# Weight conversion moved to two batches' tiles, an order edge on VectorE, and 18 identity products on TensorE

## The chip, the cores and the metric

One core of one Trainium2 chip runs the kernel. The metric is the time of the whole program on the device in microseconds. A profile is one further execution with the hardware profiler on.

## The reference, cut to what matters

```
a = softmax(phi) over the 32 slots            # (4, 8, 576, 32)
k_m, v_m = a^T k, a^T v                       # per head: 32 x 64
attn = softmax(q k_m^T / 8) v_m               # (4, 8, 576, 64)
x  = attn as 2304 tokens x 512
y1 = relu(x @ w_in)^2 @ w_out                 # first MLP,  512 -> 2048 -> 512
h  = y1 @ w_in2
out = (h * tanh(softplus(h))) @ w_out2        # second MLP, 512 -> 2048 -> 512
```

q, k, v and phi are float32; the four weight matrices arrive as 64-bit floats.

## The kernel before, in words

**Weights.** Class `Conv` turns a weight matrix into float32 in 16 units of 128 x 512 ("i1" is the first MLP's input matrix, "o1" its output matrix, "i2" and "o2" those of the second MLP). A unit takes: one load of 512 KB of raw words (L167, issued by SyncE, three buffers), a Prelu on ScalarE (L192) that scales the high word, a shift on VectorE (L214), a shift-or on VectorE (L221); for all but i1 also the split into a rounded high part on ScalarE (L187, type fp32r) and the low part on VectorE (L229). One `tick` starts a unit, does the bit operations of the unit started a tick earlier and the split of the one before that. Units of o1 stay in SBUF. Units of i2 and o2 are written from a staging tile (pool Y, tag `i1`, four buffers) to DRAM (L231) and read back later by `load_w2` (L713). The four buffers of tag `i1` are also those of the weight pages of the first input matrix: its halves `win` and the weight pages `win1r` that `load_page` (L592) reads back from DRAM.

**First MLP with attention.** `attn_unit` computes the softmax of 288 tokens of one batch ("half") and leaves it as high part `ah` (ScalarE, L375) and low part `al` (VectorE, L376). `w_part` (L386 to L393) multiplies v_m into two 128-column blocks of w_in, which gives `wp`, also as high and low part. `a_tile` then does, for each of a range of 16 blocks `fc`: six products `h` (L471 to L473) of 288 columns, Relu and Square on ScalarE (L479, L480), the split `g` into two parts (L484 or L486 on ScalarE or, for batch 3, VectorE; L487 on VectorE), and three blocks later (LAG) twelve products into four accumulators `a` (L433 to L435). `evac_y1` stores y1 to DRAM.

Batches 0 and 1 share their weights: twelve `a_tile` calls (blocks 0 to 3, 4 to 9, 10 to 15, each for both batches and both halves). They are called the first, second and third group below. Then come batch 2, halves 0 and 1, and batch 3, halves 0 and 1, with all 16 blocks each. Beside these products run the attention of later halves and the memory of later batches (`kv_unit`), a step per block. The converter `c1` (i1 and o1) runs in the first two groups; `c2` (first all of i2, then all of o2) in the third group and in batch 2, with a start in two of three ticks. In batch 3 nothing is converted; i2 is read back from DRAM in its first half, o2 in its second.

**Second MLP.** 2304 tokens in five tiles of 512 or 384, 16 blocks each: twelve products `hb` (L780 to L782), the activation on three engines, twelve or nine products `b` (L755 to L757).

**Order of the work.** A planner orders each engine's instructions by a simulated time line, so program order is not the order on the engine. `behind(marks, key)` adds an edge: the instructions in its block stand behind the marked one on the same engine. `c1.after` places the converter's VectorE work behind `marks[b, half]`; `kv_soft` of batch 2 (the maximum of phi, L260) stands behind `marks[1, 1]`. With `paced`, a Prelu stands behind the last Relu. All loads and stores are issued by SyncE, in one queue in its order. Each engine runs its own queue in order.

Of the kernel before, what the change touches and what calls it, by code (L numbers as in the profile page):

```python
# [8 lines left out]
F32 = mybir.dt.float32  # L9
F32R = mybir.dt.float32r  # L10
# [7 lines left out]
B, H, S, D, M = 4, 8, 576, 64, 32  # L18
DM, FF = 512, 2048
P = 128  # L20
# [4 lines left out]
NF = FF // P  # L25
# [4 lines left out]
LAG = 3  # L30
# [5 lines left out]
def body(tc, q, kvm, kvt, phi, w_in1, w_out1, w_in2, w_out2, out):  # L36
    nc = tc.nc
# [94 lines left out]
    wt = {}  # L132

    w1 = dram.tile([NPG, P, 4, 256], F32, name="w_i1")
    w2 = {key: dram.tile([NF, P, 2, 512], F32, name=f"w_{key}") for key in ("i2", "o2")}

# [11 lines left out]
    class Conv:  # L150
# [20 lines left out]
        def tick(self, start=True, between=None):  # L171


            ends = [x for x in self.flight if x[2] == 2]
            bits = [x for x in self.flight if x[2] == 1]
            for x in ends:
                key, u = x[0], x[1]
                if key[1] == "2":
                    x[4] = Y.tile([P, 2, 512], F32R, tag="i1", name=f"st_{key}_{u}", bufs=4)
                    x[4] = [x[4][:, 0], x[4][:, 1], x[4]]  # L180
                else:
                    if (key, u // 2) not in wt:
                        wt[key, u // 2] = tuple(
                            wo.tile([P, 2, DM], F32R, tag=f"wo{part}{u // 2}", name=f"{key}{part}{u // 2}")
                            for part in "hl")
                    x[4] = [w[:, u % 2, :] for w in wt[key, u // 2]]
                nc.scalar.copy(x[4][0], x[3])  # L187
            if start and self.started < min(self.loaded, self.limit) and self.ready(*self.order[self.started]):
                key, u = self.order[self.started]
                high = self.raw[key, u][:, :, 1].bitcast(F32)  # L190
                with behind(marks, "step" if self.paced else None):
                    nc.scalar.activation(high, high, AF.Prelu, scale=2.0 ** -112, alpha=-2.0 ** 32)  # L192
                self.started += 1
                self.flight.append([key, u, 0, None, None])
            with behind(marks, self.after):
                self.fields(bits, ends, between)
            for x in self.flight:
                x[2] += 1
            for x in list(self.flight):
                if x[2] == 3 or (x[2] == 2 and x[0] == "i1"):  # L200
                    self.done.add((x[0], x[1]))
                    self.flight.remove(x)

        def fields(self, bits, ends, between):
            for x in bits:
                key, u, c = x[0], x[1], x[1] % 2
                if key == "i1":
                    if c == 0:
                        wt[key, u // 2] = Y.tile(
                            [P, 4, 256], F32, tag="i1", name=f"win1_{u // 2}", bufs=4)  # L210
                    x[3] = wt[key, u // 2][:, :, c * P:(c + 1) * P]
                else:
                    x[3] = X.tile([P, 512], F32, tag="ct", name=f"ct_{key}_{u}", bufs=2)
                nc.vector.tensor_scalar(  # L214
                    out=x[3].bitcast(I32), in0=self.word(x, 0), scalar1=29, scalar2=None,
                    op0=ALU.logical_shift_right)
            if between is not None:
                between()
            for x in bits:
                d = x[3].bitcast(I32)  # L220
                nc.vector.scalar_tensor_tensor(  # L221
                    out=d, in0=self.word(x, 1), scalar=3, in1=d,
                    op0=ALU.logical_shift_left, op1=ALU.bitwise_or)
                if x[0] == "i1" and x[1] % 2:
                    nc.sync.dma_start(w1[x[1] // 2], wt["i1", x[1] // 2])
                self.raw.pop((x[0], x[1]))
                self.load()
            for x in ends:
                nc.vector.tensor_sub(x[4][1], x[3], x[4][0].bitcast(F32))  # L229
                if x[0][1] == "2":  # L230
                    nc.sync.dma_start(w2[x[0]][x[1]], x[4][2].bitcast(F32))  # L231

        def word(self, x, i):
            t = self.raw[x[0], x[1]][:, :, i]
# [8 lines left out]
    def bank(tag, name):  # L243
        return psum.tile([P, 512], F32, tag=tag, name=name)
# [10 lines left out]
    def kv_soft(b, p):  # L255

        ph = phi_t[p][:, at[p]:at[p] + S]
        mx = Y.tile([P, 1], F32, tag="mx", name=f"mx{b}{p}", bufs=2)
        with behind(marks, (1, 1) if b == 2 else None):
            nc.vector.tensor_reduce(out=mx, in_=ph, op=ALU.max, axis=AX.X, negate=True)  # L260
        rc = Y.tile([P, 1], F32, tag="rc", name=f"rc{b}{p}", bufs=2)
        nc.scalar.activation(ph, ph, AF.Exp, bias=mx, accum_out=rc)
        rc_t[p] = rc
# [75 lines left out]
    def attn_unit(b, half, nxt=None):  # L339
# [13 lines left out]
        for p in range(2):  # L353
# [11 lines left out]
        nc.vector.tensor_mul(xv, xv, sm.unsqueeze(2).to_broadcast([P, 2 * TB, NB]))  # L365
        yield
        a = Y.tile([P, 2, T], F32, tag="at", name=f"at{n}", bufs=1)
        marks[b, half] = nc.vector.transpose(
            a.rearrange("p a t -> p (a t)"), x.rearrange("p a t -> p (a t)"))
        pool = Y if b in (1, 2) else X  # L370
        a_t[b, half] = tuple(
            pool.tile([P, 2, T], F32R, tag=f"a{part}", name=f"a{part}{b}{half}", bufs=2)
            for part in "hl")
        hi, lo = a_t[b, half]
        nc.scalar.copy(hi, a)  # L375
        nc.vector.tensor_sub(lo, a, hi.bitcast(F32))  # L376
        yield

    wp = {}
# [1 line left out]
    def w_part(b, j, lo, hi):  # L381

        ps = banks2(f"pw{b}{j}{lo}")[:, :, :hi - lo]
        for g in range(4):
            for p in range(2):
                nc.tensor.matmul(  # L386
                    ps[M * g:M * g + M, p], vT[b][D * p:D * p + D, M * g:M * g + M],
                    wt["i1", j][D * p:D * p + D, g, lo:hi], start=True, stop=True)
        if (b, j) not in wp:
            wp[b, j] = page([P, 2, 2, 256], F32R, f"wp{b}{j}")  # L390
        t = wp[b, j]
        nc.scalar.copy(t[:, 0, :, lo:hi], ps)
        nc.vector.tensor_sub(t[:, 1, :, lo:hi], ps, t[:, 0, :, lo:hi].bitcast(F32))  # L393
# [45 lines left out]
    def evac_y1(b, half, first, last):  # L439
# [15 lines left out]
                nc.sync.dma_start(y1[:, dm - 1:dm + 1, c0:c0 + T], y1s[slot, dm // 2])  # L455
        return f

    def a_tile(b, half, f0, f1, tick, mid, post, banks=("mm",)):

        acc = [psum.tile([P, 512], F32, tag=f"acc{d}", name=f"a{b}{half}{f0}{d}") for d in range(4)]  # L460
# [2 lines left out]
        for fc in range(f0, f1):  # L463
# [4 lines left out]
            key = ahead.get((b, half, fc))  # L468
            for hg in range(2):
                with behind(done_pe, key if hg == 0 else None):  # L470
                    nc.tensor.matmul(ph, w[:, 0, hg, fs], hi[:, hg], start=(hg == 0), stop=False)  # L471
                nc.tensor.matmul(ph, w[:, 0, hg, fs], lo[:, hg], start=False, stop=False)  # L472
                nc.tensor.matmul(ph, w[:, 1, hg, fs], hi[:, hg], start=False, stop=(hg == 1))  # L473
            tick(fc)
            flush()
# [41 lines left out]
    for _ in range(N_WARM):  # L517
        nc.tensor.matmul(warm[:, :P], ident, ident, start=True, stop=True)

    kv_soft(0, 0)  # L520
    kv_soft(0, 1)
    kv_turn(0, 0, ("acc0", "acc1"))
# [10 lines left out]
    kv_mem(0, 1, (1,), "acc0")  # L533
    c1.tick()
    kv_heads(0, (1,), "acc1")
    next(at00)
    w_part(0, 0, 0, P)
    next(at00)
    c1.tick()
    c1.after = (0, 0)  # L540
# [29 lines left out]
    def attn_later(b, half):  # L570
        def nxt():
# [11 lines left out]

    subs = [(f0, f1, b, half) for f0, f1 in zip(bounds, bounds[1:])
            for b in range(2) for half in range(2)]
    c2 = Conv([("i2", u) for u in range(NF)] + [("o2", u) for u in range(NF)],
              lambda i: (Y, "raw", 3))

    def load_page(j):

# [4 lines left out]
    for i, (f0, f1, b, half) in enumerate(subs):  # L595
# [26 lines left out]
        def tick(fc):  # L622
            if len(c1.done) < 2 * NF:
                c1.tick()
            elif f0 == bounds[-2]:
                if not c2.loaded:
                    c2.load(3)
                c2.tick(start=fc % 3 != 2)

        def mid(fc):  # L630
            run_step(lanes, n_steps)
# [29 lines left out]


    def tick2(fc):
        c2.tick(start=fc % 3 != 2)

    b, nb = 2, 3
    lanes = [attn_later(b, 1), [[iter(range(2)), 2]] + kv_later(nb)]
# [25 lines left out]
    drain(*lanes)  # L693


    while len(c2.done) < 2 * NF:
        c2.tick()
    close(cm_psum2)
    cm_psum2 = tc.tile_pool(name="psum3", bufs=1, space=PSUM)
# [5 lines left out]
        tiles.append((c, n))  # L705
        c += n

    def load_w2(key, u):
        if key == "i2":
            t = Y2.tile([P, 2, 512], F32R, name=f"i2_{u}")  # L710
        else:
            t = wo.tile([P, 2, 512], F32R, tag=f"wo{'hl'[u % 2]}{u // 2}", name=f"o2_{u}")
        nc.sync.dma_start(t.bitcast(F32), w2[key][u])  # L713
        wt[key, u] = t

    y_raw, y_t = {}, {}

# [12 lines left out]
        nc.scalar.copy(hi, t)  # L730
        (nc.gpsimd if i else nc.vector).tensor_sub(lo, t, hi.bitcast(F32))  # L731

    def post0(fc):
        load_w2("i2", fc)

    def post1(fc):
        if fc >= 8 and fc % 2 == 0:
            load_y(0, fc // 2 - 4)
        elif fc >= 8:
            split_y(0, fc // 2 - 4)  # L740
        if fc >= LAG + 1 and fc % 2 == 0:
            load_w2("o2", fc - LAG - 1)
            load_w2("o2", fc - LAG)

    nothing = lambda fc: None
    acc_tags = ["mm", "b0", "bg1", "bg2"]
    a_tile(B - 1, 0, 0, NF, nothing, nothing, post0, acc_tags)
    a_tile(B - 1, 1, 0, NF, nothing, nothing, post1, acc_tags)


    def mm4_step(acc, fc, gh, gl, n, done):
# [18 lines left out]
    for i, (c0, n) in enumerate(tiles):  # L770
        acc = [psum.tile([P, 512], F32, tag=f"acc{d}", name=f"b{i}{d}") for d in range(n // P)]
        done = store_out(c0)
        for fc in range(NF):
# [9 lines left out]
            if step == 1:  # L783
                flush()
                run_pend(0)
                for c in range(NF):
                    if ("o2", c) not in wt:
                        load_w2("o2", c)
            u = X.tile([P, 512], F32, tag="ah", name=f"u{m}", bufs=2)[:, :n]
            nn = X.tile([P, 512], F32, tag="al", name=f"n{m}", bufs=2)[:, :n]  # L790
            nh = X.tile([P, 512], F32, tag="ys0", name=f"nh{m}", bufs=2)[:, :n]
# [80 lines left out]
```

## Time and profile before

| | |
|---|---|
| three runs | median 811.53 us, from 810.93 to 815.98 |
| profiled execution | 809.73 us, its span 807.9 us |
| mean granted TensorE clock | 0.983 |
| busy share: TensorE, weight load, VectorE, ScalarE, GpSimd | 96%, 84%, 72%, 56%, 15% |

The span in 40 slices of about 20 us; digits are tenths:

```profile
PE   5797999999988999999999999999999999999997
DVE  4988646785677883334588887888878887777774
PEclk7698999999999999999999999999999999999999
DMA  9991435699789977506630002000110001001001
```

PE is TensorE, DVE VectorE, ACT ScalarE, POOL GpSimd, SP SyncE. PEclk is the granted clock: whole at 2.4 GHz, half at 1.2 GHz. TensorE is below nine tenths in the first two slices, in the fourth, in slices twelve and thirteen, and in the last. The two MLPs meet at about 397 us.

### The profile page before, as it was taken

Reading aid. Unit: us, or ns where it says so; the run is one execution under the profiler, and the core shown is the slowest. Engines: PE = TensorE matmul, PEld = TensorE weight load, DVE = VectorE, ACT = ScalarE, POOL = GpSimd, SP = SyncE. Lnnn points to the kernel's source line nnn. Section 1 sums busy time; section 2 is a strip of 40 time slices with the busy share of each in tenths; the row PEclk is TensorE's granted clock in tenths of the full one; section 3 lists DMA queues with packets and bytes.
Section 4 is the critical chain, followed back from the end, with each engine's and each line's share of the span. In section 5 each row is a group of like instructions: output and inputs, shape, how many; then the busy total and the mean of one; then the engine's idle time right before and its main releaser. Section 6 shows DMA issues by size and latency. Waiting matters only on the chain.

```text
span 807.9 us, 13777 instructions
## 1 busy us (share of the span) xinstructions
PE 776.5 (96%) x5288; PEld 676.5 (84%) x5288; DVE 577.8 (72%) x1022; ACT 452.3 (56%) x916; POOL 119.4 (15%) x104
## 2 busy tenths in 40 slices
PE   5797999999988999999999999999999999999997
PEld 4586898999777988999988888888888889999896
DVE  4988646785677883334588887888878887777774
ACT  3767766785657775334445445444564446555453
POOL 0000000000000000000223243222522242222222
PEclk7698999999999999999999999999999999999999
DMA  9991435699789977506630002000110001001001
GB/s 337 406 391 73 164 100 162 235 329 362 251 312 345 389 253 281 211 1 228 248 105 1 0 27 73 0 1 1 39 53 1 0 20 54 1 1 39 1 2 39
DMA packets 38705, 111.77 MB, mean 138 GB/s; under 512 B 3952, under 2 KB 10096, under 8 KB 38640
## 3 DMA queue, kind: packets, MB, share of 16 engines
q1 hardware_dynamic: 38640, 110.90, 37.8%
q8 instruction: 41, 0.67, 0.3%
q14 instruction: 24, 0.20, 0.1%
HBM read 80.48 MB, written 30.41 MB: 137 GB/s over the span
## 4 chain that ended last, share of the span: by engine, by line
PE 80%; DMA 8%; DVE 7%; ACT 3%; issue 1%; SPq 0%; ACTq 0%; DVEq 0%
PE hb L781 8%; PE hb L780 8%; PE hb L782 8%; PE b L756 8%; PE b L755 8%; PE b L757 8%; PE a L433 6%; PE a L435 6%; PE a L434 6%; DMA raw_i<-in_moe_w_in_dram 3%; PE h L471 3%; PE h L472 3%; PE h L473 3%; DMA w_i<-st_i 2%; PE pw L386 1%
## 5 line engine op out<-in xcount | busy, mean ns | idle before, releaser
L433 PE MATMUL a<-g,o1h 128*128 128x288 f32 x512 | 150.3, 301 | 3.0 <-ACT g L484 1.5
L434 PE MATMUL a<-g,o1l 128*128 128x288 f32 x512 | 149.2, 297 | 0.0
L808 POOL TENSOR_TENSOR gl<-nh,gh 128x512 fp32r<-128x512 f32 (+1 forms) x80 | 97.4, 1219 | 285.5 <-PE b L757 177.0
L435 PE MATMUL a<-g,o1h 128*128 128x288 f32 x512 | 134.8, 295 | 0.7 <-DVE g L487 0.7
L781 PE MATMUL hb<-yl,i 128*128 128x512 f32 (+1 forms) x320 | 118.9, 372 | 0.0
L780 PE MATMUL hb<-yh,i 128*128 128x512 f32 (+1 forms) x320 | 118.9, 372 | 0.0
L782 PE MATMUL hb<-yh,i 128*128 128x512 f32 (+1 forms) x320 | 118.8, 371 | 0.0
L804 DVE SCALAR_TENSOR_TENSOR n<-n,u 128x512 f32<-128x512 f32 (+1 forms) x80 | 79.5, 994 | 52.5 <-ACT u L800 52.5
L756 PE MATMUL b<-o,gh 128*128 128x512 f32 x288 | 113.6, 395 | 0.0
L755 PE MATMUL b<-o,gh 128*128 128x512 f32 x288 | 113.5, 394 | 0.0
L757 PE MATMUL b<-o,gl 128*128 128x512 f32 x288 | 112.4, 395 | 0.0
L433 PEld LDWEIGHTS a<-g,o1h 128*128 128x128 f32 x512 | 96.5, 189 | 11.1 <-ACT g L484 4.0
L794 ACT ACTIVATE u<-hb 128x512 f32<-128x512 f32 (+1 forms) x80 | 44.4, 555 | 107.5 <-PE hb L782 107.5
L434 PEld LDWEIGHTS a<-g,o1l 128*128 128x128 f32 x512 | 96.8, 189 | 1.3 <-issue 1.2
L479 ACT ACTIVATE s<-h 128x288 f32<-128x288 f32 x128 | 52.0, 410 | 79.9 <-PE h L473 78.4
L435 PEld LDWEIGHTS a<-g,o1h 128*128 128x128 f32 x512 | 90.7, 188 | 3.0 <-DVE g L487 1.6
L471 PE MATMUL h<-ah,wp 128*128 128x288 f32 x256 | 79.9, 313 | 5.3 <-ACT s L479 2.6
L472 PE MATMUL h<-al,wp 128*128 128x288 f32 x256 | 77.8, 304 | 5.3 <-DVE al L376 5.3
L487 DVE TENSOR_TENSOR g<-s,g 128x288 fp32r<-128x288 f32 x128 | 59.9, 469 | 32.2 <-ACT g L484 30.3
L731 POOL TENSOR_TENSOR yl<-yr,yh 128x512 fp32r<-128x512 f32 (+1 forms) x16 | 21.3, 1345 | 396.2 <-PE h L473 391.4
L807 ACT CAST gh<-nh 128x512 fp32r<-128x512 f32 (+1 forms) x80 | 46.3, 579 | 57.4 <-DVE nh L806 54.3
L473 PE MATMUL h<-ah,wp 128*128 128x288 f32 x256 | 77.1, 301 | 0.0
(98 smaller groups left out, 1393.4 us busy)
## 6 DMA issues: line engine op xcount, KB each, us to landing
raw_i<-in_moe_w_in_dram SPq DMA_DIRECT2D x32, 512.0 KB, 5.2
raw_o<-in_moe_w_out_dram SPq DMA_DIRECT2D x32, 512.0 KB, 7.7
win1r<-w_i SPq DMA_DIRECT2D x17, 512.0 KB, 5.8
w_i<-st_i SPq DMA_DIRECT2D x16, 512.0 KB, 4.5
w_o<-st_o SPq DMA_DIRECT2D x16, 512.0 KB, 6.8
i<-w_i SPq DMA_DIRECT2D x16, 512.0 KB, 7.7
o<-w_o SPq DMA_DIRECT2D x16, 512.0 KB, 4.1
kv<-in_kvm_dram SPq DMA_DIRECT2D x5, 1024.0 KB, 8.8
```

Source lines behind the costliest of these rows:

```text
L433: nc.tensor.matmul(o, wh[:, c, cs], sh, start=first, stop=False)
L434: nc.tensor.matmul(o, wl[:, c, cs], sh, start=False, stop=False)
L435: nc.tensor.matmul(o, wh[:, c, cs], sl, start=False, stop=last)
L471: nc.tensor.matmul(ph, w[:, 0, hg, fs], hi[:, hg], start=(hg == 0), stop=False)
L472: nc.tensor.matmul(ph, w[:, 0, hg, fs], lo[:, hg], start=False, stop=False)
L473: nc.tensor.matmul(ph, w[:, 1, hg, fs], hi[:, hg], start=False, stop=(hg == 1))
L755: nc.tensor.matmul(acc[t], gh[:, cs], wh, start=(fc == 0), stop=False)
L756: nc.tensor.matmul(acc[t], gh[:, cs], wl, start=False, stop=False)
L757: nc.tensor.matmul(acc[t], gl[:, cs], wh, start=False, stop=(fc == NF - 1))
L780: nc.tensor.matmul(h, wh[:, d * P:d * P + P], yh, start=(d == 0), stop=False)
L781: nc.tensor.matmul(h, wh[:, d * P:d * P + P], yl, start=False, stop=False)
L782: nc.tensor.matmul(h, wl[:, d * P:d * P + P], yh, start=False, stop=(d == 3))
```

## The change

i2 and o2 are no longer converted by one converter. `c2` converts o2 alone, in the tiles of batch 2, a start every second block; its first three loads are issued in the last `a_tile` of the third group. Its staging tiles are two tiles of 128 x 512 (one for each part) under the tags `ys2` and `ys3` of pool Y, two buffers each, and each part is stored by a DMA of its own. A new converter `c3` converts i2 in the tiles of batch 3, straight into the SBUF tiles that the second MLP reads; the DRAM copy of i2, its stores and its read-back are gone. Both are paced. `marks[b, half]` is now the low part `al` (L376) and no longer the transpose before it (L368). `keep_warm` issues products of the identity with itself behind a given TensorE instruction: four behind a transpose of `kv_heads`, five behind the first `w_part`, five and four behind the first two products of the first `a_tile`.

```
-    w2 = {key: dram.tile([NF, P, 2, 512], F32, name=f"w_{key}") for key in ("i2", "o2")}
+    w2 = dram.tile([NF, P, 2, 512], F32, name="w_o2")
...
-                if key[1] == "2":
-                    x[4] = Y.tile([P, 2, 512], F32R, tag="i1", name=f"st_{key}_{u}", bufs=4)
-                    x[4] = [x[4][:, 0], x[4][:, 1], x[4]]
+                if key == "i2":
+                    t = wt[key, u] = Y2.tile([P, 2, 512], F32R, name=f"i2_{u}")
+                    x[4] = [t[:, 0], t[:, 1]]
+                elif key == "o2":
+                    x[4] = [Y.tile([P, 512], F32R, tag=f"ys{i}", name=f"st{i}_{u}", bufs=2) for i in (2, 3)]
...
-                if x[0][1] == "2":
-                    nc.sync.dma_start(w2[x[0]][x[1]], x[4][2].bitcast(F32))
+                if x[0] == "o2":
+                    for i in range(2):
+                        nc.sync.dma_start(w2[x[1], :, i], x[4][i].bitcast(F32))
...
-        marks[b, half] = nc.vector.transpose(
-            a.rearrange("p a t -> p (a t)"), x.rearrange("p a t -> p (a t)"))
+        nc.vector.transpose(a.rearrange("p a t -> p (a t)"), x.rearrange("p a t -> p (a t)"))
...
-        nc.vector.tensor_sub(lo, a, hi.bitcast(F32))
+        marks[b, half] = nc.vector.tensor_sub(lo, a, hi.bitcast(F32))
...
+    def keep_warm(ins, n):
+        with tc.issue_after(ins.ins):
+            for _ in range(n):
+                nc.tensor.matmul(warm2[:, :P], ident, ident, start=True, stop=True)
...
+                if n == "00_0" and hg == 0:
+                    keep_warm(one, 5)
...
+                if n == "00_0" and hg == 0:
+                    keep_warm(one, 4)
...
+    keep_warm(done_pe["pkt", 0], 4)
     next(at00)
     w_part(0, 0, 0, P)
+    keep_warm(done_pe["pw"], 5)
...
-    c2 = Conv([("i2", u) for u in range(NF)] + [("o2", u) for u in range(NF)],
-              lambda i: (Y, "raw", 3))
+    c2 = Conv([("o2", u) for u in range(NF)], lambda i: (Y, "raw", 3))
+    c3 = Conv([("i2", u) for u in range(NF)], lambda i: (Y2, "raw", 3))
+    c2.paced = c3.paced = True
...
-            elif f0 == bounds[-2]:
-                if not c2.loaded:
-                    c2.load(3)
-                c2.tick(start=fc % 3 != 2)
+            elif final and not c2.loaded:
+                c2.load(3)
...
     def tick2(fc):
-        c2.tick(start=fc % 3 != 2)
+        c2.tick(start=fc % 2 == 0)
...
+    c3.load(3)
+
+    def tick3(fc):
+        c3.tick(start=fc % 2 == 0)
...
-    def post0(fc):
-        load_w2("i2", fc)
...
-    a_tile(B - 1, 0, 0, NF, nothing, nothing, post0, acc_tags)
-    a_tile(B - 1, 1, 0, NF, nothing, nothing, post1, acc_tags)
+    a_tile(B - 1, 0, 0, NF, tick3, nothing, nothing, acc_tags)
+    a_tile(B - 1, 1, 0, NF, tick3, nothing, post1, acc_tags)
+    while len(c3.done) < NF:
+        c3.tick()
```

## Rows read from the trace of the kernel before

**Rows 1.** Windows by stage: stretch, its length, busy us (instructions) by engine, clock, DMA, GB/s

```profile
...
70.96:83.16 12.20, 7.97 (x52) 7.16 (x53) 11.03 (x26) 8.63 (x22) 0.00 (x0) 0.72 0.16 51
...
150.44:221.53 71.09, 68.84 (x635) 63.02 (x633) 46.80 (x101) 48.42 (x114) 0.00 (x0) 1.00 0.86 305
221.53:277.46 55.93, 50.02 (x513) 44.02 (x513) 45.04 (x92) 38.10 (x85) 0.00 (x0) 1.00 0.93 341
277.46:320.31 42.85, 42.85 (x407) 38.20 (x406) 25.27 (x49) 29.96 (x70) 0.00 (x0) 1.00 0.77 287
...
358.58:396.77 38.19, 38.19 (x291) 38.19 (x289) 16.79 (x38) 18.30 (x42) 3.90 (x4) 1.00 0.58 206
396.77:807.90 411.13, 406.64 (x1862) 342.75 (x1860) 324.86 (x484) 204.41 (x352) 114.61 (x93) 1.00 0.08 27
```

**Rows 2.** Chain of waits, 220 to 262 us: start, us, what

```profile
...
225.07 7.06 DMA w_i<-st_i
...
247.67 9.32 DMA w_o<-st_o
257.07 0.62 ACT st_o L187
...
258.54 0.40 PE h L471
...
```

**Rows 3.** Waits of ScalarE, 150.4 to 277.5 us: who for whom, us, times, longest

```profile
ACT raw_o L192 <- DMA raw_o<-in_moe_w_out_dram: 8.3, 4, 2.8
ACT raw_i L192 <- DMA raw_i<-in_moe_w_in_dram: 7.1, 8, 1.6
...
ACT st_o L187 <- DMA w_o<-st_o: 4.5, 2, 3.8
...
```

**Rows 4.** Time line of TensorE, 70 to 81 us: start, us, instruction, idle before it

```profile
70.96 0.53 PE L471 MATMUL h<-ah,wp 128*128 128x288 f32 x2 [0.37 <-ACT ah L375]
75.72 0.61 PE L472 MATMUL h<-al,wp 128*128 128x288 f32 x1 [4.23 <-DVE al L376]
...
80.87 0.66 PE L386 MATMUL pw<-win,vT 64*32 64x256 f32 x16
```

**Rows 5.** Time line of VectorE, 69 to 79 us

```profile
69.43 0.78 DVE L368 STREAM_TRANSPOSE at<-x 128x576 f32<-128x576 f32 x1
...
72.04 1.41 DVE L260 TENSOR_REDUCE mx<-phi 128x1 f32<-128x576 f32 x2
...
74.92 0.75 DVE L376 TENSOR_TENSOR al<-at,ah 128x576 fp32r<-128x576 f32 x1
...
78.33 0.69 DVE L221 SCALAR_TENSOR_TENSOR win<-raw_i,win 128x512 int32<-128x512 int32 x1 [0.50 <-ACT raw_i L192]
```

**Rows 6.** Windows of the two stretches at half clock

```profile
12.00:32.48 20.48, 12.17 (x164) 7.99 (x165) 17.54 (x37) 11.61 (x24) 0.00 (x0) 0.50 1.04 403
...
73.44:80.27 6.83, 4.55 (x19) 4.55 (x20) 6.14 (x17) 4.56 (x13) 0.00 (x0) 0.50 0.07 27
```

**Rows 7.** Time line of TensorE at the start

```profile
1.52 3.78 PE L518 MATMUL warm<-ident 128*128 128x128 f32 x16 [1.52 <-POOL ident masks.py:199]
...
22.42 0.61 PE L471 MATMUL h<-ah,wp 128*128 128x288 f32 x1 [1.14 <-ACT wp L392]
...
24.13 0.61 PE L472 MATMUL h<-al,wp 128*128 128x288 f32 x1 [1.10 <-DVE al L376]
```

**Rows 8.** A conversion unit's instructions: durations in ns, least/median/most

```profile
L192 ACT ACTIVATE raw_i<-raw_i x32: 651/676/705, 12.6 to 190.4; 128x512 f32<-128x512 f32 x32
...
L187 ACT CAST st_i<-ct_i x16: 604/622/637, 143.5 to 228.6; 128x512 fp32r<-128x512 f32 x16
...
L214 DVE TENSOR_SCALAR ct_i<-raw_i x16: 417/422/429, 140.8 to 222.2; 128x512 int32<-128x512 int32 x16
L221 DVE SCALAR_TENSOR_TENSOR ct_i<-raw_i,ct_i x16: 682/686/695, 141.8 to 222.9; 128x512 int32<-128x512 int32 x16
L229 DVE TENSOR_TENSOR st_i<-ct_i,st_i x16: 681/688/694, 145.2 to 229.6; 128x512 fp32r<-128x512 f32 x16
```

More of the change, by code (lines that the diff above doesn't have):

```diff
@@ L385, in w_part @@
             for p in range(2):
-                nc.tensor.matmul(
+                done_pe["pw"] = nc.tensor.matmul(
                     ps[M * g:M * g + M, p], vT[b][D * p:D * p + D, M * g:M * g + M],
@@ L470, in a_tile @@
                 with behind(done_pe, key if hg == 0 else None):
-                    nc.tensor.matmul(ph, w[:, 0, hg, fs], hi[:, hg], start=(hg == 0), stop=False)
-                nc.tensor.matmul(ph, w[:, 0, hg, fs], lo[:, hg], start=False, stop=False)
+                    one = nc.tensor.matmul(ph, w[:, 0, hg, fs], hi[:, hg], start=(hg == 0), stop=False)
+                if n == "00_0" and hg == 0:
+                    keep_warm(one, 5)
+                one = nc.tensor.matmul(ph, w[:, 0, hg, fs], lo[:, hg], start=False, stop=False)
+                if n == "00_0" and hg == 0:
+                    keep_warm(one, 4)
                 nc.tensor.matmul(ph, w[:, 1, hg, fs], hi[:, hg], start=False, stop=(hg == 1))
@@ L518, in body @@
         nc.tensor.matmul(warm[:, :P], ident, ident, start=True, stop=True)
+    warm2 = bank("b0", "warm2")
     kv_soft(0, 0)
@@ L693, in body @@
     drain(*lanes)
-    while len(c2.done) < 2 * NF:
+    while len(c2.done) < NF:
         c2.tick()
@@ L706, in body, with load_w2 @@
         c += n
[L708 to L714, printed above, removed]
+    def load_w2(u):
+        t = wo.tile([P, 2, 512], F32R, tag=f"wo{'hl'[u % 2]}{u // 2}", name=f"o2_{u}")
+        nc.sync.dma_start(t.bitcast(F32), w2[u])
+        wt["o2", u] = t
+    c3.load(3)
+    def tick3(fc):
+        c3.tick(start=fc % 2 == 0)
     y_raw, y_t = {}, {}
@@ L741, in post1 @@
         if fc >= LAG + 1 and fc % 2 == 0:
-            load_w2("o2", fc - LAG - 1)
-            load_w2("o2", fc - LAG)
+            load_w2(fc - LAG - 1)
+            load_w2(fc - LAG)
     nothing = lambda fc: None
     acc_tags = ["mm", "b0", "bg1", "bg2"]
-    a_tile(B - 1, 0, 0, NF, nothing, nothing, post0, acc_tags)
-    a_tile(B - 1, 1, 0, NF, nothing, nothing, post1, acc_tags)
+    a_tile(B - 1, 0, 0, NF, tick3, nothing, nothing, acc_tags)
+    a_tile(B - 1, 1, 0, NF, tick3, nothing, post1, acc_tags)
+    while len(c3.done) < NF:
+        c3.tick()
     def mm4_step(acc, fc, gh, gl, n, done):
@@ L787, in body @@
                     if ("o2", c) not in wt:
-                        load_w2("o2", c)
+                        load_w2(c)
             u = X.tile([P, 512], F32, tag="ah", name=f"u{m}", bufs=2)[:, :n]
```

## Prediction

> **What bounds the kernel now.** I read the windows by stage first [rows 1]. From 277 us on TensorE is busy without a break to the tail of the second MLP (42.85 of 42.85, 38.19 of 38.19, 406.64 of 411.13), so nothing can be won there and something could be lost. It stands idle in three earlier places that the change touches: 4.23 us in 70.96 to 83.16 (12.20 less 7.97; the last `a_tile` of the first group), 2.25 us in the third group (71.09 less 68.84) and 5.91 us in the first half of batch 2 (55.93 less 50.02). The sum is 12.39 us. The reader is to see that in the last of these VectorE is busy for 45.04 of 55.93 us and the DMA engines for 0.93 of the time.
>
> Then the chain of waits in that stage [rows 2]: it runs through the staging of the converted weights. A store to DRAM takes 7.06, a later one 9.32 us, and only then can ScalarE round the next unit into the freed buffer (257.07), behind which the Relu waits that `h` on TensorE needs (258.54). The wait list [rows 3] says the same of ScalarE, whose queue is in order: 8.3 us in 4 waits and 7.1 us in 8 for raw words, 4.5 us in 2 for a staging store.
>
> Last the first group. At 70.96 TensorE starts `h` with the high part of the softmax and then stands for 4.23 us until 75.72, for the low part [rows 4]. The transpose before it ended at 70.21 (69.43 and 0.78), but VectorE subtracts the low part at 74.92 only, after conversion work and the two maxima of phi [rows 5]. While TensorE stood there the granted clock fell to its lower level, 1.2 GHz, from 73.44 to 80.27 [rows 6].
>
> **The change part by part.**
>
> *Low part before other VectorE work.* The conversion's bit operations and the maxima that were tied behind the transpose are now tied behind the low part. It needs the high part, which TensorE reads at 70.96 [rows 4], so it can start near 71.1 in place of 74.92, 3.8 us sooner. What is queued behind it on VectorE is the work that ran in those 3.8 us; it is only moved. Its end matters: VectorE's merge of the next weight page starts at 78.33 and ends at 79.02 (0.69), and `pw`, which reads it, started at 80.87 because TensorE came late. If the merge stays where it is, `pw` comes 1.85 us sooner: the lower bound. The upper bound is the whole wait and the clock: 4.23 us, and half of the 4.55 us that TensorE worked at half clock [rows 6], together 6.5 us. VectorE is busy for 11.03 of the stage's 12.20 us [rows 1], so I take a value near the lower bound: **2.5 us**. The other low parts of the first group cost less: TensorE waited 1.10 us for that of the first half [rows 7]. But VectorE, which is busy for 17.54 of 20.48 us there [rows 6], will now stand while ScalarE casts (0.7 us, as between 70.21 and 70.96). I take 0.5 us for these, between a loss of 0.7 and a gain of 1.1.
>
> *Eighteen identity products.* Eight of them at the start were 16 instructions and 3.78 us at half clock [rows 7], so 0.47 each; 18 take 8.5 us at 1.2 GHz and half of that, 4.25, at 2.4. TensorE's idle there before the second `h` product is some 2.2 us in the two rows shown (1.14 and 1.10) [rows 7], and the products stand ahead of real work in its queue. If the clock stays low they delay `h` by up to 8.5 less 2.2, 6.3 us; VectorE's backlog hides part of that. If the clock rises before 32.48 they give back: TensorE was busy for 12.17 us at half clock [rows 6], of which half, 6.1 us, is the most that can come back. Both ends are cut by VectorE, busy all but 2.9 us of that stretch, on whose work the chain depends. I take **0**, the middle, with plus and minus 4 as ends after that cut.
>
> *No conversion in the third group.* All ticks of `c2` there go, with their raw loads, stores and ScalarE waits [rows 3]; SyncE's queue holds weight-page loads, attention loads and three raw loads alone. What is left is attention, memory and `w_part`. I take the idle, 2.25 us, nearly whole: **2 us**. Ends: 0.5 (attention's own waits) and 4 (small gaps that a busy row doesn't show).
>
> *o2 in batch 2, half the rate.* A unit costs ScalarE 0.676 and 0.622 us and VectorE 0.422, 0.686 and 0.688 [rows 8], 1.30 and 1.80. In 16 blocks 8 units start in place of 11, so VectorE loses 5.4 of 45.04 us. The weight-page buffers are no longer shared with staging; a store waits for the low part on SyncE, and behind it stand raw and weight-page loads, as before. Two stores of 256 KB replace one of 512 KB, so SyncE issues twice as many. The idle of 5.91 us should go, and a little that the busy rows hide: **6 us**, ends 2 and 8. In the second half of batch 2 the conversion now lasts to the end; before it was idle-free with 25.27 of 42.85 us on VectorE, and I cost it at 0.5 us lost.
>
> Here a rule can be set against the rows. By matmul busy time the last two parts hold 2.25 and 5.91 us. The Trainium skill, "Perfetto Trace Analysis", section "Identifying the Most-Contended Engine", says that matmul busy time is not a good measure for TensorE and that the busy share of weight loads is to be used. By that, with the idle-free 38.20 of 42.85 us as the full rate, 44.02 us of loads are 49.4 us of work and leave 6.5 us, and the third group's 63.02 us are 70.7 and leave 0.4: the sum of the two parts would be 6.9 us by the rule and is 8 by mine.
>
> *i2 in batch 3.* Eight units per half add 10.4 us to ScalarE and 14.4 to VectorE: 28.7 and 31.2 of 38.19 us in the busier half [rows 1]. The products of the other blocks hide that; if the cover is gone, ScalarE is the next bound. The DRAM write and the read of 8 MB go; 16 raw loads of 512 KB take the place of the 16 read-backs. The first loads wait until pool Y's buffers come free, and a Prelu that waits holds the Relu behind it. I take **0.5 us** lost, ends 0 and 4.
>
> *The sum.* 2.5 + 0.5 + 0 + 2 + 6 - 0.5 - 0.5 = 10 us off the profiled execution's 809.73, which is 799.7. The median of the runs is 1.8 us above that execution, so **801.5 us**.
>
> **The rivals.**
>
> *VectorE holds, not staging (about 806).* In the first half of batch 2 the attention of two halves and the memory of batch 3 stay, VectorE keeps 39.6 us of work, and the moved work of the first group only changes place. Then the parts give 1.85, 0, 0.5 to 1 and 2 to 3: 5.5 us, 806. For it: VectorE's 45.04 of 55.93. Against it: the chain there goes through stores, not through VectorE's own work [rows 2].
>
> *All of the loss comes back (about 793).* 6.5, 1.1, 4 and 8 us, with nothing lost later, is 19.6; the products would have to raise the clock for no price. For it: batch 2's second half ran idle-free with conversion [rows 1]. Against it: VectorE in the first group.
>
> *The two staging buffers are too few (about 826, the other side).* Place: ScalarE's rounding of o2 unit u, which now waits for the store of unit u-2, where the old ring had four buffers. Two units are four blocks, 9.6 us at 38.19 us for 16 blocks. A buffer is held for 0.62, 0.69 and the store; with a store of 9.32 us [rows 2] that is 10.6, 1 us too long, and with a queue ahead of it on SyncE it can reach the 3.8 us that ScalarE once waited [rows 3]. It decides from stores of over 8.3 us on. At 2.4 us each, 14 units make 34 us; ScalarE's idle in the second half (42.85 less 29.96) takes up 13; 21 less the 5 us won elsewhere is 16 lost, 826. Against it: fewer bytes move at once than at a DMA share of 0.93. The Trainium skill, "DMA: Bandwidth & Descriptors", section "Anatomy of one DMA", puts a fixed 2 us on each DMA (it measured another queue kind), by which two halves cost 2 us more than the whole and the point would come sooner; no run here shows it.
>
> *It does not do what it says*: the planner may leave the low part late, or the clock may stay low under the products. That is the first rival's case.
>
> **How the numbers follow.** Forecast 0.50, 796 to 807 for itself; VectorE holds 0.30; all comes back 0.13; too few buffers 0.07. The range 794 to 810 leaves out the last, some of the third and the ends of the second. A change of 1% is about what a measurement tells from none: 803.4 and below is faster. Of the forecast three quarters lie there (0.38), of the second a fifth (0.06), of the third all (0.13): 0.57 faster, 0.38 within 1%, 0.05 slower.
>
> **What would show it.** In the changed profile: the low part of batch 1, half 1, within 1 us of its cast, and no half-clock stretch near 73 to 80 us; TensorE idle under 1 us in the third group and under 2 us in batch 2's first half; no chain through staging stores; batch 3's two halves still 38.2 us each. Wrong would be: ScalarE waits on staging stores in batch 2, batch 3 over 39 us a half, or `h` of the first half later than 24.1 us with the clock still low after it.

## The result and the profile after

The changed kernel takes 801.12 us (median of four runs, 799.65 to 802.12) against 811.23 before; ratio 0.9862, 95% interval 0.9821 to 0.9903. On a second chip it was 801.53, ratio 0.9893 (0.9873 to 0.9912). The forecast was 801.5. The medians of the first chip are 10.1 us apart. The profiled execution's span fell from 807.9 to 799.2 us. Line numbers moved: `h` is now L479, L482 and L485, `a` L435 to L437, Relu L491, the Prelu L194, the merge L223, the low part L378, `pw` L388.

Windows by stage, cut where a tile's first `h` starts. First those of the kernel before that [rows 1] lacks (first tile to the second tile of the second group, then to the third group):

```profile
70.96:99.73 28.77, 24.54 (x176) 22.00 (x177) 21.98 (x50) 21.26 (x52) 0.00 (x0) 0.88 0.38 129
99.73:150.44 50.71, 50.71 (x416) 44.87 (x415) 29.85 (x62) 33.44 (x77) 0.00 (x0) 1.00 0.44 145
```

Then the changed kernel, same columns:

```profile
71.67:99.68 28.01, 24.35 (x192) 21.00 (x193) 22.80 (x50) 20.96 (x52) 0.00 (x0) 0.94 0.40 132
99.68:148.68 49.00, 49.00 (x391) 44.38 (x389) 26.28 (x56) 31.13 (x72) 0.00 (x0) 1.00 0.41 130
148.68:216.91 68.23, 67.78 (x639) 62.31 (x637) 29.24 (x66) 37.00 (x87) 0.00 (x0) 1.00 0.39 127
216.91:267.88 50.97, 50.77 (x518) 44.49 (x517) 34.83 (x69) 32.80 (x72) 0.00 (x0) 1.00 0.85 273
267.88:311.15 43.27, 43.27 (x411) 38.62 (x409) 32.13 (x61) 35.12 (x81) 0.00 (x0) 1.00 0.75 251
311.15:349.40 38.25, 38.25 (x297) 38.25 (x289) 26.62 (x60) 23.78 (x52) 0.00 (x0) 1.00 0.45 146
349.40:387.58 38.18, 38.18 (x290) 38.18 (x289) 26.20 (x60) 22.88 (x51) 0.00 (x0) 1.00 0.75 261
387.58:799.18 411.60, 406.63 (x1862) 342.50 (x1860) 323.11 (x484) 206.51 (x358) 119.32 (x96) 1.00 0.09 29
```

Read the ends. At the second tile of the second group the two kernels stand within 0.05 us of each other (99.73, 99.68). The changed kernel has by then issued 16 instructions more (192 for 176 in the rows), all of them `pw`, some 0.7 us of work: that is all that the first group gave in this execution. Then 1.71 us come until the third group, 2.86 in it (71.09 to 68.23), 4.96 in batch 2's first half (55.93 to 50.97), less 0.42 in its second, 0.03 in batch 3, and 0.47 go in the second MLP. That is the 8.7 us. TensorE's idle fell from 2.25 to 0.45 us in the third group and from 5.91 to 0.20 in batch 2's first half, where VectorE's work fell from 45.04 to 34.83 us and the DMA share from 0.93 to 0.85. Batch 3 carries all of i2 at the old length. ScalarE's waits from 148.7 to 267.9 us no longer name a load or a store [rows 3]; its longest two groups now are:

```profile
ACT s L491 <- PE h L485: 26.8, 27, 3.5
ACT phi L265 <- DVE kk L311: 4.9, 2, 3.2
```

The first group deserves a closer look, because what was foreseen there did happen. Time line of TensorE of the changed kernel, the rows that answer to [rows 4], and one later:

```profile
71.67 0.54 PE L479 MATMUL h<-ah,wp 128*128 128x288 f32 x2 [0.68 <-ACT ah L377]
72.46 0.40 PE L482 MATMUL h<-al,wp 128*128 128x288 f32 x1 [0.26 <-DVE al L378]
78.56 0.67 PE L388 MATMUL pw<-win,vT 64*32 64x256 f32 x16 [0.45 <-DVE win L223]
...
91.79 0.40 PE L479 MATMUL h<-ah,wp 128*128 128x288 f32 x1 [2.33 <-ACT s L491]
```

The wait for the low part is 0.26 us in place of 4.23, the half-clock stretch near 73 us is gone, and `pw` starts 2.31 us sooner. Then TensorE stands 2.33 us before 91.79. The chain of waits says why:

```profile
83.81 0.61 DVE win L223
84.42 0.02 issue
84.43 5.97 DMA raw_o<-in_moe_w_out_dram
...
90.42 0.03 ACT raw_o L194
...
90.99 0.44 ACT s L492
91.43 0.31 ACT s L491
...
91.79 0.40 PE h L479
```

A raw load can go out only when VectorE's merge has freed a buffer (84.42); it takes 5.97 us; the Prelu that needs it holds ScalarE, and the Relu behind it holds TensorE. After that stand the clock falls. The two stretches at half clock of the changed kernel, which answer to [rows 6]:

```profile
14.84:25.08 10.24, 7.81 (x88) 6.94 (x89) 8.80 (x21) 5.18 (x9) 0.00 (x0) 0.50 1.03 404
...
93.35:96.76 3.41, 3.41 (x27) 2.31 (x26) 2.22 (x5) 2.36 (x6) 0.00 (x0) 0.50 0.50 171
```

So in this execution most of the order edge's 2.3 us was given back before 100 us. (Two runs below, whose first group is the same, keep it.) The full clock at the start came 7.4 us sooner (25.08 in place of 32.48) and gave nothing that shows: between these two times VectorE is busy for 7.36 of 7.40 us and TensorE for 5.93, and the second tile starts at 44.70 in place of 43.65.

### The profile page after: what moved, and what is told of

The parts are those of the page before. It is cut to its first block, busy times and chain, and to the rows that moved or that the text cites. A ratio compares the mean times of both kernels' runs of the same rounds, so it can differ in the third digit from the quotient of the medians.

```text
span 799.2 us, 13772 instructions
## 1 busy us (share of the span) xinstructions
PE 776.8 (97%) x5324; PEld 678.8 (85%) x5324; DVE 575.3 (72%) x1022; ACT 454.5 (57%) x916; POOL 120.2 (15%) x104
## 4 chain that ended last, share of the span: by engine, by line
PE 88%; DVE 4%; DMA 3%; ACT 3%; issue 1%; SPq 0%; ACTq 0%; DVEq 0%
PE hb L796 8%; PE hb L795 8%; PE hb L797 8%; PE b L771 8%; PE b L770 8%; PE b L772 8%; PE a L435 8%; PE a L436 8%; PE a L437 7%; PE h L479 4%; PE h L482 4%; PE h L485 4%; PE pw L388 2%; DMA raw_i<-in_moe_w_in_dram 2%; PE pk L306 1%
## 5 line engine op out<-in xcount | busy, mean ns | idle before, releaser
L435 PE MATMUL a<-g,o1h 128*128 128x288 f32 x512 | 149.7, 299 | 0.5 <-ACT g L496 0.4
L437 PE MATMUL a<-g,o1h 128*128 128x288 f32 x512 | 135.5, 296 | 0.0
L435 PEld LDWEIGHTS a<-g,o1h 128*128 128x128 f32 x512 | 96.3, 188 | 6.4 <-ACT s L491 3.3
L491 ACT ACTIVATE s<-h 128x288 f32<-128x288 f32 x128 | 52.4, 412 | 73.3 <-PE h L485 69.4
L437 PEld LDWEIGHTS a<-g,o1h 128*128 128x128 f32 x512 | 91.0, 189 | 2.8 <-DVE g L499 1.1
L479 PE MATMUL h<-ah,wp 128*128 128x288 f32 x256 | 78.9, 310 | 4.7 <-ACT s L491 3.9
L482 PE MATMUL h<-al,wp 128*128 128x288 f32 x256 | 76.0, 297 | 0.3 <-DVE al L378 0.3
L485 PE MATMUL h<-ah,wp 128*128 128x288 f32 x256 | 75.5, 296 | 0.0
```

The source lines that it names most:

```text
L435: nc.tensor.matmul(o, wh[:, c, cs], sh, start=first, stop=False)
L437: nc.tensor.matmul(o, wh[:, c, cs], sl, start=False, stop=last)
L479: one = nc.tensor.matmul(ph, w[:, 0, hg, fs], hi[:, hg], start=(hg == 0), stop=False)
L482: one = nc.tensor.matmul(ph, w[:, 0, hg, fs], lo[:, hg], start=False, stop=False)
```

## Experiments

The starts of each kernel's stages (first `h` of the stage, us from the span's start) are what most verdicts rest on. Each comes from one execution, and the old staging ring below shows that executions whose first group is the same can lie 2.4 us apart at the first of these points:

| kernel | 2nd group, 2nd tile | 3rd group | batch 2 | its 2nd half | batch 3 | second MLP |
|---|---|---|---|---|---|---|
| before | 99.73 | 150.44 | 221.53 | 277.46 | 320.31 | 396.77 |
| changed | 99.68 | 148.68 | 216.91 | 267.88 | 311.15 | 387.58 |
| changed, second chip | 99.52 | 148.51 | 216.72 | 268.84 | 312.10 | 388.54 |
| weights only | 99.67 | 149.38 | 217.58 | 268.77 | 312.03 | 388.47 |
| no products | 100.48 | 149.48 | 217.69 | 268.39 | 311.65 | 388.09 |
| order edge only | 98.38 | 148.15 | 219.08 | 277.28 | 320.13 | 396.59 |
| o1 low on GpSimd | 101.04 | 150.06 | 217.51 | 269.35 | 312.61 | 389.05 |
| old staging ring | 97.17 | 146.18 | 214.40 | 264.49 | 309.72 | 386.85 |
| o2 in third group | 97.17 | 146.14 | 223.95 | 274.22 | 316.96 | 393.40 |
| short conversion | 94.61 | 143.64 | 211.88 | 263.94 | 307.20 | 383.64 |
| four raw buffers | 96.73 | 146.44 | 214.66 | 266.33 | 309.59 | 386.03 |
| six low parts on GpSimd | 97.26 | 146.26 | 214.49 | 266.03 | 309.29 | 385.73 |
| both of these | 97.25 | 146.95 | 215.17 | 266.70 | 309.96 | 386.40 |

**The parts by themselves (one chip, before 810.85 us).**

The weights' move alone:

```
-    keep_warm(...)                      # all four calls
-        marks[b, half] = nc.vector.tensor_sub(lo, a, hi.bitcast(F32))
+        marks[b, half] = nc.vector.transpose(...)
```

> The changed kernel without the order edge on the low part and without the identity products: the moved weight conversion alone. Theory W (all of the gain comes from the moved conversion, since at 99.7 us the changed kernel stood where the old one stood): 800 to 802.5 us, about 1.2% under the kernel before. Rival F (the first group's earlier low part is worth the 2.5 to 3 us that I forecast and something else took them back): 803 to 805 us.

Measured 802.22 us (801.44 to 803.21), ratio 0.9904 (0.9881 to 0.9927). Theory W holds. TensorE waits the old 4.23 us for the low part, and yet the second tile of the second group starts at 99.67. From there to batch 3 it gains 8.2 us on the kernel before, nearly all of the change.

Without the products:

```
-    keep_warm(...)                      # all four calls, the order edge stays
```

> The changed kernel without the 18 identity products, with the order edge. Theory W (products worth nothing, because VectorE's work and not the clock sets the first group's pace): within 1 us of the changed kernel's 801.1, with half clock again until about 32 us. Rival F2 (the earlier full clock is worth its 6.1 us bound less the delay of the first h): 803 to 805 us. Rival F3 (the products only delay the first h by 1.5 us): 799.5 to 800.

Measured 802.32 (800.62 to 803.70), ratio 0.9903 (0.9881 to 0.9926). The span's first `h` starts at 22.72 in place of 23.90, half clock lasts to 31.35 us and comes once more to 38.17, and the stage table shows 0.8 us lost by 100 us. That is within what executions differ by, and the median is 0.8 and 1.2 us above the two of the changed kernel on other chips, so the products' worth is about 1 us at most and stays open. The 803 to 805 us of rival F2 are not what was measured, though two of the six runs (803.27 and 803.70) reach into them.

The order edge alone, on the kernel before:

```
-        marks[b, half] = nc.vector.transpose(...)
+        nc.vector.transpose(...)
...
+        marks[b, half] = nc.vector.tensor_sub(lo, a, hi.bitcast(F32))
```

> The kernel before with the order edge alone (the conversion and the maxima stand behind the low part). Theory W: 810 to 812 us, no change, although the 4.23 us wait for the low part near 71 us is gone; TensorE then waits 2 to 4 us later, between 85 and 100 us. Rival F: 807.5 to 809 us.

Measured 809.09 (805.43 to 814.13), ratio 0.9984 (0.9963 to 1.0005): no change that can be told from none; the median lies between what theory W and what rival F expected. The profiled execution is 1.35 us ahead at the second group, where TensorE has stood again before 91.93 us for 2.11 us, as foreseen, and 2.45 us ahead at batch 2. In batch 2's first half it then takes 2.27 us longer than the kernel before. Its idle time is only 0.45 us longer (6.36 for 5.91); the rest is busy time, at half clock from 257.72 to 261.13:

```profile
219.08:277.28 58.20, 51.84 (x514) 45.60 (x513) 44.78 (x92) 38.14 (x85) 0.00 (x0) 0.97 0.94 336
```

**What in batch 2 and the third group (second chip, before 810.97 us, changed 801.53).**

> The changed kernel again, as the base for the other three on the same chip: 800 to 802.5 us, the second group's second tile starting near 99.7 us.

o2's staging back in the old ring:

```
-    x[4] = [Y.tile([P, 512], F32R, tag=f"ys{i}", ..., bufs=2) for i in (2, 3)]
+    x[4] = Y.tile([P, 2, 512], F32R, tag="i1", ..., bufs=4)
...
-    for i in range(2): nc.sync.dma_start(w2[x[1], :, i], ...)
+    nc.sync.dma_start(w2[x[1]], ...)
```

> The changed kernel with o2's staging back in the four buffers that the weight pages also use, one store of 512 KB a unit; what is converted where stays changed. Theory R (the shared buffers, through which ScalarE waits for stores and weight pages, cost batch 2 its 5.9 us of idle): batch 2's first half 53.5 to 56 us in place of 51.0, total 803 to 806. Rival A (the amount of conversion and DMA beside it cost them, and the ring only showed it): first half 50.5 to 51.5, total 800 to 802.5.

Measured 800.74 (799.21 to 802.08), ratio 0.9886 (0.9866 to 0.9905). Theory R fails as the main cause. The ring does hold ScalarE again, and TensorE stands 2.87 us in batch 2's second half. The windows of batch 2, and ScalarE's waits in it:

```profile
214.40:264.49 50.09, 50.09 (x523) 44.84 (x521) 35.19 (x70) 33.16 (x73) 0.00 (x0) 1.00 0.72 245
264.49:309.72 45.23, 42.36 (x391) 38.05 (x390) 30.88 (x59) 34.00 (x80) 0.00 (x0) 1.00 0.74 260
```

```profile
ACT s L491 <- PE h L485: 13.0, 13, 3.5
ACT st_o L190 <- DMA w_o<-st_o: 8.1, 5, 4.1
```

Batch 2 takes 95.32 us in all, against 95.38 with the new buffers on this chip, but leaves one `pw` (16 instructions) to batch 3, whose first half takes 38.94 us for 38.26. From batch 2 to the second MLP it is 172.45 us here, 171.82 and 170.67 in the two executions of the changed kernel, and 175.24 before. So 2.8 of the 3.4 to 4.6 us won there remain with the old ring: most of it is the lighter conversion, and the ring is worth 0.6 to 1.8 us. Which part of the lighter conversion counts (VectorE's work, ScalarE's or the DMA traffic) no run separates.

The same run says something of the first group that the first profile hid. It differs from the changed kernel in o2's staging alone, which is not in use before batch 2, and in both traces VectorE, ScalarE and SyncE have the same instructions in the same order up to 97 us. Yet it starts the second group's second tile at 97.17, 2.35 us sooner than the changed kernel on the same chip. The changed kernel's window and its TensorE after the stand, then the old ring's:

```profile
72.14:99.52 27.38, 24.29 (x193) 21.36 (x193) 22.80 (x50) 20.98 (x52) 0.00 (x0) 0.94 0.41 135
91.66 0.61 PE L479 MATMUL h<-ah,wp 128*128 128x288 f32 x1 [1.71 <-ACT s L491]
```

```profile
71.46:97.17 25.71, 22.90 (x193) 20.08 (x193) 22.27 (x50) 20.84 (x52) 0.00 (x0) 1.00 0.44 143
90.71 0.40 PE L479 MATMUL h<-ah,wp 128*128 128x288 f32 x1 [1.48 <-ACT s L491]
```

Both stand for the late load; only the first falls to half clock behind it (from 91.58 to 94.99). The two are 0.95 us apart before the stretch and 2.35 behind it. The next run has the same first group too: it stands 1.70 us, keeps the full clock and reaches 97.17 as well. So the edge, with the products, gains between nothing and 2.6 us at the second group, as the clock falls after that stand or not.

o2's conversion started in the third group (old ring, i2 still in batch 3):

```
-            elif final and not c2.loaded:
-                c2.load(3)
+            elif f0 == bounds[-2]:
+                if not c2.loaded:
+                    c2.load(3)
+                c2.tick(start=fc % 2 == 0)
```

> The changed kernel with o2's staging in the old four buffers as in the run before, and its conversion started in the third group at the same half rate: 12 units there, 4 in batch 2. i2 stays beside batch 3. If the third group's 2.9 us come from having no conversion there, that group goes back from 68.2 to 70.5 or 71 us and batch 2's first half to about 51: total 802 to 804. If conversion at half rate hides in the third group too, 68.2 to 69 us, total 800 to 802.

Measured 806.88 (803.99 to 808.91), ratio 0.9953 (0.9937 to 0.9970). The third group takes 77.81 us, longer than the 71.09 of the kernel before and than I expected; batch 2 then takes 93.0. From the third group to the second MLP it takes 247.26 us, the old ring 240.67, so conversion in the third group costs 6.6 us in this form. How much of that is the work itself stays open. Part of it is a queue on SyncE: the load of phi for batch 3 goes out at 194.33 behind a weight page and a staging store, and VectorE can read it at 202.80, 8.5 us later (3.7 in the old-ring run); TensorE stands 3.26 us for what follows and then works at half clock from 204.50 to 207.91. Time line of SyncE, then waits in the third group:

```profile
193.40 0.33 SPq L608 DMA_DIRECT2D win1r<-w_i  x1
193.83 0.41 SPq L234 DMA_DIRECT2D w_o<-st_o  x1
194.33 0.39 SPq L76 DMA_DIRECT2D phi<-in_phi_dram  x1
```

```profile
ACT phi L265 <- DVE mx L263: 7.8, 1, 7.8
DVE mx L263 <- DMA phi<-in_phi_dram: 6.5, 2, 3.9
...
PE psc L348 <- ACT kT L322: 3.3, 1, 3.3
```

**What holds the first group.**

All low parts of o1 on GpSimd:

```
-    nc.vector.tensor_sub(x[4][1], x[3], ...)
+    (nc.gpsimd if x[0] == "o1" else nc.vector).tensor_sub(x[4][1], x[3], ...)
```

> The changed kernel with the low parts of o1 (16 subtractions of 0.69 us) on GpSimd in place of VectorE. Theory V (VectorE's amount of work holds the first group, so that an order edge only moves the wait): 797 to 799.5 us, with less lost before 100 us. Rival D (the late raw words hold it, whose load waits for a free buffer): 800 to 802 us, no change. If GpSimd's subtraction is late itself, TensorE waits for the low part of o1 and the time is above 802.

Measured 800.64 (798.82 to 802.17), ratio 0.9882 (0.9859 to 0.9904), and 101.04 us at the second group. By its expectation this spoke for rival D, but it did not decide: one subtraction takes 1.41 us on GpSimd on average, the first (at 26.47) 2.54; VectorE waits 1.2 us for it, TensorE then stands 2.60 us before 32.29 and works at half clock from 31.82 to 38.65. So two things changed at once.

Less work on VectorE, none put elsewhere. The first converter leaves out the three low bits of i1 and o1:

```
-    nc.vector.tensor_scalar(..., op0=ALU.logical_shift_right)
-    nc.vector.scalar_tensor_tensor(..., op0=ALU.logical_shift_left, op1=ALU.bitwise_or)
+    nc.vector.tensor_scalar(out=d, in0=self.word(x, 1), scalar1=3, ..., op0=ALU.logical_shift_left)
```

> The changed kernel whose first converter (i1 and o1) leaves out the three low bits: no right shift (0.42 us) and a left shift of one input in place of the merge (0.42 for 0.69), so 0.69 us less of VectorE's work in each of 32 units, some 14 us less before 100 us. Theory V (the amount of VectorE's work holds the first group): the second group's second tile starts at 95 to 97.5 in place of 99.7 us, total 796.5 to 799. Rival O (order and single late waits hold it, not the amount): 98.5 to 100.5, total 800 to 802.5.

Measured 796.83 (795.10 to 797.32), ratio 0.9832 (0.9812 to 0.9853): theory V holds, within limits. Its window up to the second group's second tile, under it the changed kernel's:

```profile
0.00:94.61 94.61, 82.82 (x941) 70.47 (x941) 63.56 (x143) 64.43 (x145) 0.87 (x8) 0.91 0.78 292
```

```profile
0.00:99.68 99.68, 82.95 (x940) 70.06 (x941) 76.84 (x169) 65.31 (x145) 0.87 (x8) 0.93 0.74 278
```

13.3 us less on VectorE end the stage 5.1 us sooner, with the same work on TensorE. Not all of the 5.1 us is the work's: no half clock comes near 91 us here, and the old ring is 2.5 us sooner for the same reason, with all of VectorE's work. The closest comparison is the next run, which has the same half clock at the start (to 26.98 us, here 26.65) and the same first `h` (25.32, here 25.39). It reaches the point 2.1 us later, all of it lost in the first three tiles (47.82 us for 45.71). So the work is worth some 2 us.

One raw buffer more, one weight-page buffer less:

```
-    (Y, "raw", 3)  ...  tag="i1", bufs=4
+    (Y, "raw", 4)  ...  tag="i1", bufs=3
```

> The changed kernel with four buffers for raw words in place of three, and three for weight pages in place of four (the room for it). Theory D (in the first group the wait that TensorE meets near 91 us is a raw load that could not be issued before VectorE's merge freed its buffer): the load goes out sooner, the 1.7 to 2.3 us wait and the half-clock stretch behind it go, the second group's second tile starts at 96.5 to 98 us, total 798 to 800. Rival: VectorE's amount of work holds it all the same, 99 to 100 us, total 800.5 to 802. If three page buffers are too few, batch 2 gets longer than 52 and 43.3 us.

Measured 799.01 (798.56 to 799.52; before 810.73 on a further chip), ratio 0.9852 (0.9827 to 0.9878). Theory D holds for the cause of the wait: with the buffer TensorE has no wait over 0.2 us between 84 and 99 us and no half clock there. From the fourth tile on it is as fast as the short conversion (windows of this run, then of that one):

```profile
73.14:96.73 23.59, 22.83 (x192) 20.08 (x193) 22.01 (x49) 20.66 (x52) 0.00 (x0) 1.00 0.42 147
71.10:94.61 23.51, 22.48 (x193) 19.99 (x193) 16.85 (x39) 21.51 (x54) 0.00 (x0) 1.00 0.50 157
```

But its 96.73 us is only 0.44 better than the old ring's 97.17, and at the third group it is not ahead (146.44 for 146.18). What the buffer takes away is the stand after which the clock can fall; that it saves more is not shown. Three page buffers cost nothing that shows in batch 2 (51.7 and 43.3 us). But from the second group's second tile to the third group it takes 49.71 us, and 49.70 with both changes below, where the changed kernel takes 49.00 with as many instructions on TensorE (391); what these 0.7 us are is not shown.

Only the six low parts that no product of the first group waits for:

```
+    (nc.gpsimd if x[0] == "o1" and 4 <= x[1] < 10 else nc.vector).tensor_sub(...)
```

> The changed kernel with the low parts of o1's units 4 to 9 alone (six subtractions of 0.69 us, none of the first group's own products waits for them) on GpSimd. Theory V (VectorE's amount): VectorE loses 4.1 us before 100 us, the second tile of the second group starts 1 to 3 us sooner, at 96.5 to 98.5, total 798.5 to 800.5. Rival: as when all of them moved, nothing is gained, 99 to 101 us.

Measured 799.37 (798.22 to 799.58), ratio 0.9853 (0.9828 to 0.9879), 97.26 us. That is inside what theory V expected, but the old ring reaches 97.17 with nothing taken from VectorE in the first group, so the run does not decide for V.

> Both of the two before together, as a version that could beat the changed kernel: by theories D and V 796.5 to 799 us, with the second tile of the second group at 95 to 97.5; by their rivals 800 to 802.

Measured 800.49 (799.46 to 801.62), ratio 0.9870 (0.9847 to 0.9894), 97.25 us: the start lies inside what was expected, the time above it. The two do not add up; each removes the wait near 91 us. None of these three is clear of the changed kernel, whose intervals on two chips overlap theirs.

## Why the prediction was right, and where not

- **The sum** (10 us) against 8.7 between the profiled spans and 10.1 between the medians: right, by terms that were in part wrong and evened out. That the forecast lies within 0.4 us of the median is luck: the profiled execution came 1.3 us above the sum's 799.7, and the 1.8 us added for the median were 0.1. (The third rival's own parts, 19.6 us, give 792 us and not 793.)
- **Low part first, 2.5 us.** The step as I put it came true at the place I named: `pw` 1.85 us sooner or more, measured 2.31. As a term of the end time it was incomplete. I said that the work behind the low part "is only moved" and did not follow it to the next thing it frees: the merge at 83.81 frees a raw buffer, and the late load costs 2.33 us and here a stretch at half clock. Measured for the whole first group, where I had 3.0: 0.7 us in this execution (0.05 at the second group and the `pw` done ahead; at the third group, with the same products done, 0.70 ahead of the weights alone), but 3.2 ahead of them in the two executions without the half clock (146.18 and 146.14 for 149.38). My size was that of an execution in which the clock does not fall, and I had not seen that it can. VectorE's amount of work, of which the first rival spoke, costs some 2 us in the first three tiles (short conversion).
- **Products, 0.** Right in size: between nothing and 1 us. They moved the first `h` by 1.48 us, inside the bounds, and in the first profile raised the clock 7.4 us sooner. That is no fixed gain: on the second chip the last stretch of half clock ended at 33.55. Of the 40 us from the start, 10.2 to 17.1 are at half clock in the nine traces with the products and 20.5 in each of the four without.
- **Third group, 2 us.** Measured 2.86, within the ends; 1.80 of it is idle time. I had nothing for the stretch before it; 1.71 us came there. The run with the weights alone gains 1.0 of it (49.71 for 50.71 us). The old i2 work had begun ahead of its group (the first rounding of i2 starts at 143.5 us [rows 8]), but TensorE was busy throughout that stretch in both, with 416 instructions before and 407 here, so part of the 1.0 is work that only moved behind the cut. The other 0.71 is TensorE's work that the edge's order had put before the stretch (391 instructions for 407): it belongs to the first group.
- **Batch 2, 6 less 0.5 us.** Measured 4.96 less 0.42, and 3.81 less 0.41 in the execution on the second chip. The idle went as forecast (0.20 us left; 1.08 on the second chip). My reason was only half right: the chain through staging stores [rows 2] led me to name the shared buffers first, and with them put back 2.8 of the 3.4 to 4.6 us remain. Most of it is less conversion beside it.
- **Weight-load share.** The rule of the Trainium skill that I cited ("Perfetto Trace Analysis", "Identifying the Most-Contended Engine") gave 6.9 us for the two parts and the matmul idle 8; measured are 2.86 and 4.96, 7.8, and on the second chip 2.88 and 3.81, 6.7. The sum does not decide between the two; part by part (0.4 and 6.5 by the rule, 2.25 and 5.91 by the idle) the idle was nearer on both chips.
- **Batch 3, 0.5 us lost.** Measured 0.03 won; the cover held, with ScalarE at 23.8 and VectorE at 26.6 of 38.25 us, less than the 28.7 and 31.2 that I had reckoned.
- **Too few staging buffers.** It did not decide: no staging store stands among ScalarE's waits in the changed profile, and one of 0.5 us on the second chip.

## What to carry to other kernels

Work that runs beside a saturated engine is free only where the helpers have room: move it to the stage with the lowest share on them, even if it must be issued later. When an order edge removes a wait, follow the work it pushes back to the next buffer that it frees; a gain of 2.3 us met a late load 12 us later, and whether it lasted hung on the clock behind that stand. A buffer took the stand away. When a chain runs through a shared ring, put the ring back before believing that it was the cause. And before a stage's start in one trace is taken for an effect, look for a run that did not touch that stage: two of them moved by 2.4 us here.

## What was not expected of the hardware

The clock can fall after small stands, and their length does not say whether: at the same place 2.33 and 1.71 us in the two executions of the changed kernel were followed by half clock (93.35 to 96.76, 91.58 to 94.99), 2.11 us in the order-edge run, 1.70 with o2 in the third group and 1.48 in the old ring were not. One such stretch cost 1.4 us (2.35 less 0.95, old ring). GpSimd took 1.41 us on average for the subtraction that VectorE does in 0.69 [rows 8]. A staging store of 256 KB took 4.8 us to land (median of 32); one of 512 KB had taken 6.8 before, but 4.5 in the old-ring run (medians of 16). So halving the store did not shorten it.
